# Gated expert rows of one token tile per pair: scaled by ScalarE and added by an accumulating DMA, instead of added by VectorE

## The chip, the cores and the metric

The kernel runs on one core of one Trainium2 chip. The metric is the device time of one execution in microseconds; the median of several executions is quoted. Those of the kernel before agree within 0.1 to 0.3%. A program on one core has no second die to be compared with, so every run here counts as "fast"; all of them are used. The profile takes one execution; its span is about 2 us shorter than the time.

Before the change: 989.57 us (median of 2 runs, 989.13 to 990.0).

## The reference, cut to what matters

A linear attention makes `x` (4608 tokens, 512 columns). Then every expert is applied to every token, weighted by a gate that a Sinkhorn iteration balances:

```python
out = np.zeros((N, D), dtype=np.float32)          # N, D, E, F = 4608, 512, 8, 1024
for e in range(E):
    h = np.maximum(x @ w1[e], 0.0)
    ye = h @ w2[e]
    out += P[:, e:e + 1] * ye                     # P: the balanced gates
```

The last line is what the change moves: a scaled addition of 512 columns per token and expert into an f32 output tile that stays in SBUF until the end.

## The kernel before

Experts 1 to 7 use a Strassen-like scheme with seven products in place of eight. Two instruction streams are woven together on TensorE: *groups* (the first matmul of the expert, 384 tokens wide, with results in the PSUM banks `X` = `h_ps`, `Y` = `copied_ps` and `Z` = `p7_ps`) and *pairs* (the second matmul, one pair of 128-token tiles `g1`, `g2` at a time). A `fill()` inside a group runs one step of a pair.

```python
    def group(hT, tw, xs, n, i, fill):
        ...
        X = ps_h[0].tile([P, TCH], FP32, name="h_ps")
        product(X, b11, x_part(0, 0, n), True)          # TensorE, 2 matmuls of 384 columns
        se.copy(out=Y[:, 0:TU], in_=X[:, 0:TU])         # ScalarE: X must be read before it grows
        fill()
        ...                                             # (last product of the group before)
        fill()
        product(X, T2, s2, False)                       # adds to X
        u2 = snapshot(X, "u2")                          # ScalarE again
        fill()
        product(Y, b21, x_part(0, 1, n), False)
        se.activation(out=h11, in_=Y[:, 0:TU], func=AF.Relu)
        fill()
        product(X, T1, s1, False)
        u4 = snapshot(X, "u4")
        ...
```

So three times in a group TensorE may not add to `X` before ScalarE has copied it out. A pair takes its seven steps at these places in the stream (seven places per pair), and gates its rows on VectorE:

```python
    OFFSETS = {"P1": 0, "P2": 3, "P7": 4, "P6": 5, "P4": 8, "P5": 9, "P3": 13}
    ...
        def add(self, g, rows, a=None):                 # class Pair
            ...
            a = acc(g) if a is None else a
            ve.scalar_tensor_tensor(
                out=a, in0=rows, scalar=P_tok[:, g, self.e : self.e + 1], in1=a,
                op0=ALU.mult, op1=ALU.add,
            )
        ...
            elif name == "P2":
                self.mult(self.W, self.a12, b21)
                self.add(self.g1, self.W, acc(self.g1)[:, 0:DH])     # half of the row, 256 columns
                ...
            elif name == "P3":
                self.mult(self.U, self.S4, b22)
                self.add(self.g1, self.U, acc(self.g1)[:, DH:Dm])    # the other half
                ...
```

The weights of the next expert come from GpSimd's DMA queue, since they are cast from f32 to f16 on the way, 1 MB (as written) at a time:

```python
            if n == 0 and e + 1 < E:
                w_next = new_weights(wA if e % 2 else wB)
                load_w1(w_next, e + 1, 1)
            if n == 2 and e + 1 < E:
                load_w2(w_next, e + 1, 1)
```

A scheduler puts the instructions of each engine into a fixed order when the program is built; TensorE's is tied to the written order, ScalarE's and VectorE's are not from expert 2 on. At run time each engine works through its own list in order.

## Time and profile before

| what | where it is read | number |
|---|---|---|
| TensorE busy in the stage of the pairs | busy time by window | 50.0 of 50 us |
| VectorE, ScalarE in the same stage | busy time by window | 43, 28 of 50 us |
| TensorE's share of the chain that ended last | chain of waits | 93% |
| TensorE waiting for gating adds | waits | 1.3 us in all |
| one pair | timeline | 6.1 us |

Busy time by engine, the first part of the profile page (busy us, share of the span, number of instructions):

```profile
PE 968.0 (98%) x7846; PEld 677.9 (69%) x7846; DVE 810.4 (82%) x1838; ACT 566.4 (57%) x1260; POOL 60.4 (6%) x82
```

Two stretches of 50 us of the stage that the change touches, from the view of busy time by window (us, then busy us and instructions of each engine, granted TensorE clock, DMA share, GB/s):

```profile
500.00:550.00 50.00, 49.98 (x384) 37.32 (x383) 43.01 (x102) 27.78 (x63) 0.75 (x1) 1.00 0.26 58
600.00:650.00 50.00, 49.98 (x383) 37.27 (x382) 43.16 (x103) 27.95 (x63) 0.75 (x1) 1.00 0.26 58
```

The first line of the chain that ended last, by engine:

```profile
PE 93%; DMA 2%; DVE 2%; ACT 1%; POOL 1%; issue 0%; DVEq 0%; POOLq 0%; ACTq 0%; SPq 0%
```

A VectorE that is busy 43 us of 50 looks like the engine to relieve. The waits view says which of the two waits for the other (engine, what it was to make, what it waited for: us in total, times, longest):

```profile
DVE acc_lo L814 <- PE rows_ps L109: 74.4, 77, 1.2
...
PE rows_ps L109 <- DVE acc_hi L814: 1.3, 3, 0.6
```

The gating adds wait 74 us for TensorE's rows, and TensorE waits 1.3 us for gating adds (all of it at `acc_hi`, the last four token tiles of the output; none at `acc_lo`). VectorE is used a great deal, and it is not what the time hangs on. The timeline (start, duration, engine, operation) around one `X` bank copy, with the lines of VectorE and of TensorE's own loading of weights (PEld) left out:

```profile
501.99 0.49 PE L109 MATMUL h_ps<-xT,w1e 128*128 128x384 f16 x2
502.32 0.60 PE L109 MATMUL rows_ps<-w2e,hs 128*128 128x256 f16 x4
502.57 0.46 ACT L763 COPY copied_ps<-h_ps 128x384 f32<-128x384 f32 x1 [0.33 <-PE h_ps L109]
502.75 0.49 PE L109 MATMUL p_ps<-xT,T 128*128 128x384 f16 x2
503.09 0.48 PE L109 MATMUL h_ps<-S,T 128*128 128x384 f16 x2
```

ScalarE's copy of `X` ends at 503.03 and TensorE's next product into `X` starts at 503.09. The starts of TensorE's products follow each other at 0.33 us (384 columns, two matmuls) and 0.43 us (256 columns, four), with no gap. ScalarE is busy only 28 us of 50, but in places like this one it has 0.06 us to spare.

The weight loads, from the list of DMA issues (KB each, median us from issue to landing):

```profile
w1e<-in_moe_w_dram POOLq DMA_DIRECT2D x7, 1024.0 KB, 9.3
w2e<-in_moe_w_dram POOLq DMA_DIRECT2D x7, 1024.0 KB, 10.0
```

### The profile page before, as it was taken

How to read it: one execution, taken by the hardware profiler on the slowest of the kernel's cores; microseconds unless marked ns; L12 is line 12 of the kernel's file. 1: busy time of each engine (PE TensorE's matmuls, PEld its weight loads, DVE VectorE, ACT ScalarE, POOL GpSimd, SP SyncE). 2: the span in 40 equal slices, each digit the busy share in tenths (PEclk: the TensorE clock that was granted, in tenths of full speed). 3: DMA queues.
4: the chain of work that ended last, by engine and by line, in shares of the span. 5: the costliest groups of instructions: out<-in, count | busy, mean ns of one | idle time of the engine just before them, and what ended most of it. 6: DMA issues, size and time to landing. Idle time of an engine off the chain costs nothing.

```text
span 987.4 us, 20228 instructions
## 1 busy us (share of the span) xinstructions
PE 968.0 (98%) x7846; PEld 677.9 (69%) x7846; DVE 810.4 (82%) x1838; ACT 566.4 (57%) x1260; POOL 60.4 (6%) x82
## 2 busy tenths in 40 slices
PE   7999999989999999999999999999999999999997
PEld 6445544447777777777777777777777777777775
DVE  5886774779889888988789888988789888988887
ACT  5756665467776555555555555555555555555551
POOL 6302110010000000000000000000000000000001
PEclk8999999999999999999999999999999999999999
DMA  9969981642013410133113400233103400104535
GB/s 168 206 99 154 160 153 26 125 67 67 26 48 68 75 42 25 38 79 67 42 33 68 88 29 25 51 66 68 49 25 68 92 25 27 48 25 114 131 86 128
DMA packets 80336, 73.54 MB, mean 74 GB/s; under 512 B 33264, under 2 KB 72176, under 8 KB 80240
## 3 DMA queue, kind: packets, MB, share of 16 engines
q0 software_dynamic: 27232, 30.94, 19.9%
q1 hardware_dynamic: 52768, 41.06, 16.9%
q8 instruction: 61, 1.00, 0.4%
q14 instruction: 35, 0.29, 0.1%
q10 hardware_dynamic: 240, 0.26, 0.1%
HBM read 83.12 MB, written 12.98 MB: 97 GB/s over the span
## 4 chain that ended last, share of the span: by engine, by line
PE 93%; DMA 2%; DVE 2%; ACT 1%; POOL 1%; issue 0%; DVEq 0%; POOLq 0%; ACTq 0%; SPq 0%
PE rows_ps L109 34%; PE h_ps L109 28%; PE copied_ps L109 11%; PE p_ps L109 11%; PE y_ps L109 5%; PE small_ps L109 4%; DMA v_ld<-in_v_dram 2%; DMA q_pT<-q_p 1%; DVE xT L109 0%; DVE acc_hi L814 0%; POOL hs_last L829 0%; DVE P_tok L109 0%; DMA out_dram<-acc_lo 0%; DVE colp L109 0%; ACT u L109 0%
## 5 line engine op out<-in xcount | busy, mean ns | idle before, releaser
L814 DVE SCALAR_TENSOR_TENSOR acc_lo<-rows_ps,P_tok,acc_lo 128x512 f32<-128x512 f32 (+1 forms) x322 | 203.7, 642 | 74.5 <-PE rows_ps L109 74.4
L109 PEld LDWEIGHTS <-H 128*128 128x128 f16 x2080 | 203.0, 98 | 83.1 <-issue 1.2
L750 ACT CAST u<-h_ps 128x384 f16<-128x384 f32 x288 | 137.8, 478 | 131.2 <-PE h_ps L109 130.6
L109 PEld LDWEIGHTS <-w1e 128*128 128x128 f16 x1632 | 156.3, 98 | 67.9 <-issue 7.8
L744 DVE CUSTOM_DVE_ANT_0 H<-p_ps,u 128x384 f16<-128x384 f32 x329 | 181.7, 552 | 6.6 <-PE p_ps L109 6.4
L109 PEld LDWEIGHTS <-hs 128*128 128x128 f16 x1500 | 146.6, 98 | 56.2
L109 PE MATMUL h_ps<-S,w1e 128*128 128x384 f16 x672 | 164.1, 326 | 1.1 <-ACT u L109 0.9
L109 PE MATMUL p_ps<-xT,T 128*128 128x384 f16 x672 | 164.1, 326 | 0.1
L109 PE MATMUL h_ps<-xT,w1e 128*128 128x384 f16 (+1 forms) x616 | 150.3, 351 | 1.4 <-DVE xT L109 1.3
L109 PE MATMUL rows_ps<-V,H 128*128 128x256 f16 x1000 | 150.0, 273 | 0.7 <-DVE acc_hi L814 0.7
L109 PE MATMUL rows_ps<-w2e,hs 128*128 128x256 f16 x1000 | 150.0, 273 | 0.0
L782 ACT ACTIVATE H<-h_ps 128x384 f16<-128x384 f32 x144 | 70.7, 491 | 95.0 <-PE h_ps L109 95.0
L109 PEld LDWEIGHTS <-T 128*128 128x128 f16 x1008 | 98.1, 98 | 29.2 <-issue 2.8
L109 PE MATMUL rows_ps<-w2e,H 128*128 128x256 f16 (+1 forms) x568 | 91.2, 285 | 0.0
L763 ACT COPY copied_ps<-h_ps 128x384 f32<-128x384 f32 x144 | 67.5, 468 | 35.2 <-PE h_ps L109 35.2
L773 ACT ACTIVATE H<-copied_ps 128x384 f16<-128x384 f32 x144 | 70.9, 492 | 20.3 <-PE copied_ps L109 20.3
L109 PE MATMUL h_ps<-S,T 128*128 128x384 f16 x336 | 81.8, 325 | 0.3 <-ACT copied_ps L109 0.3
L109 PE MATMUL copied_ps<-xT,w1e 128*128 128x384 f16 x336 | 82.1, 326 | 0.0
L109 PE MATMUL copied_ps<-w2e,H 128*128 128x256 f16 x504 | 75.5, 272 | 0.0
L109 PE MATMUL rows_ps<-V,hs 128*128 128x256 f16 x500 | 75.0, 272 | 0.0
L814 DVE SCALAR_TENSOR_TENSOR acc_lo<-copied_ps,P_tok,acc_lo 128x256 f32<-128x256 f32 x126 | 60.3, 479 | 0.4
L814 DVE SCALAR_TENSOR_TENSOR acc_hi<-rows_ps,P_tok,acc_hi 128x512 f32<-128x512 f32 (+1 forms) x56 | 41.3, 738 | 20.1 <-PE rows_ps L109 19.3
(135 smaller groups left out, 957.5 us busy)
## 6 DMA issues: line engine op xcount, KB each, us to landing
S<-x_saved SPq DMA_DIRECT2D x108, 192.0 KB, 2.4
out_dram<-acc_lo SPq DMA_DIRECT2D x62, 128.0 KB, 2.4
w1e<-in_moe_w_dram POOLq DMA_DIRECT2D x7, 1024.0 KB, 9.3
w2e<-in_moe_w_dram POOLq DMA_DIRECT2D x7, 1024.0 KB, 10.0
k_ld<-in_k_dram POOLq DMA_DIRECT2D x16, 288.0 KB, 8.4
v_ld<-in_v_dram POOLq DMA_DIRECT2D x16, 288.0 KB, 9.4
q_ld<-in_q_dram POOLq DMA_DIRECT2D x16, 288.0 KB, 7.8
x_saved<-S SPq DMA_DIRECT2D x18, 192.0 KB, 1.9
```

The lines of the kernel that those rows point to most:

```text
L109: i = getattr(self.engine, name)(*args, **kwargs)
L744: latest = ve._custom_dve(TENSOR_ADD_SAT, out=out, in0=ps[:, 0:TU], in1=t[:], s0=FP32_MAX, s1=0.0)
L750: se.copy(out=t[:], in_=ps[:, 0:TU])
L763: se.copy(out=Y[:, 0:TU], in_=X[:, 0:TU])
L773: se.activation(out=h11, in_=Y[:, 0:TU], func=AF.Relu)
L782: se.activation(out=h12, in_=X[:, 0:TU], func=AF.Relu)
L814: ve.scalar_tensor_tensor(out=a, in0=rows, scalar=P_tok[:, g, self.e : self.e + 1], in1=a, op0=ALU.mult, op1=ALU.add,)
```

## The change

The intent: take work from VectorE, the engine second in use. For experts 2 to 6, `g1` of each pair is no longer added by VectorE. ScalarE writes the gate times the rows into an SBUF tile `gated` (two buffers), and when both halves are there, a DMA from GpSimd's queue adds the tile to the output tile.

```diff
+    g_pool = ctx.enter_context(tc.tile_pool(name="g_pool", bufs=2))
...
+            self.by_dma = 1 < e < E - 1
...
+        def gate_half(self, cols, rows):
+            se.activation(
+                out=self.gated[:, cols], in_=rows, func=AF.Copy,
+                scale=P_tok[:, self.g1, self.e : self.e + 1],
+            )
...
             elif name == "P2":
                 self.mult(self.W, self.a12, b21)
+                if self.by_dma:
+                    self.gated = g_pool.tile([P, Dm], FP32, name="gated")
+                    self.gate_half(slice(0, DH), self.W)
+                    return
                 self.add(self.g1, self.W, acc(self.g1)[:, 0:DH])
...
             elif name == "P3":
                 self.mult(self.U, self.S4, b22)
+                if self.by_dma:
+                    self.gate_half(slice(DH, Dm), self.U)
+                    nc.gpsimd.dma_start(
+                        out=acc(self.g1), in_=self.gated[:], accum_op=ALU.add
+                    )
+                    return
                 self.add(self.g1, self.U, acc(self.g1)[:, DH:Dm])
```

## The prediction

> **What bounds the kernel now.** TensorE. In the stage that the change touches (expert pairs, about 240 to 980 us) the table of engine busy time by window shows TensorE 49.97 to 50.00 us busy in every 50 us, VectorE 41 to 45, ScalarE about 28, GpSimd 0 to 1.6. The chain of waits is 93% PE. The timeline shows its products (0.33 us for 384 columns, 0.43 for 256) back to back. In the waits view VectorE waits 94 us for row products and TensorE 1.3 us for the gating adds: relieving VectorE is worth at most a few us.
>
> **What the change removes, adds, moves.** 5 experts x 18 pairs = 90 pairs. Off VectorE: 180 adds of 128x256 at 0.48 us = 86 us (41-45 falls to about 36 per 50). Onto ScalarE: 180 scaled copies of 128x256, 0.36 us each like the present copy of that shape, = 65 us (28 rises to about 33 per 50). New: 90 accumulating 256 KB DMAs from GpSimd (+23.6 MB), one per 6.1 us. The PE order is unchanged.
>
> **What lies on the critical path.** The new loop through two buffers: the first scaled half of pair k+2 (step P2) waits in ScalarE's in-order queue until the DMA of pair k has landed. From the end of P3 of pair k to the end of P2 of pair k+2 the present timeline gives 3.4 to 3.7 us; less the copy (0.37) about 3.0 us remain for the DMA.
> The DMA: present weight loads start their first packet 1.5 to 1.7 us after GpSimd's issue and take 0.17 us per 2 KB row; 8 rows per engine 1.4 us, plus receipt and semaphores 0.5: about 3.6 us (estimate), more if accumulating slows the rows. The Trainium skill, "DMA: Bandwidth & Descriptors", "Anatomy of one DMA", gives 2.0 us + bytes/436e3 = 2.6 us for a plain copy; no run shows it yet. So ScalarE is blocked perhaps 0.6 to 0.9 us per pair, up to 2 us with slow accumulation. TensorE feels it where a snapshot of the h bank follows: those have only 0.1 or 0.5 us of slack. Estimate: 5 to 90 us in all, central 25.
> Second: the weight loads share GpSimd's queue (one only, by "SWDGE vs HWDGE vs iDMA" there). They take 9.4 and 10.4 us to land; a P3 comes 1.7 us after a w1 load's issue and another just after a w2 load's. Those accumulations wait behind 1 MB; ScalarE blocks 5 to 8 us, eight times (4 w1 + 4 w2): about 40 us.
>
> **Prediction.** 1055 us, range 1005 to 1130. Faster by over 2%: 0.01; within 2%: 0.12; slower by over 2%: 0.87.
>
> **What would show it.** (1) VectorE busy falls by some 86 us and its idle time grows: no gain. (2) ScalarE waits for the DMA into the output tile: a new entry, tens of us, with the longest single waits 5 us or more, just after weight issues. (3) Landing of the accumulation: median 3 to 5 us, maximum over 9. (4) TensorE idle waiting for ScalarE (the h-bank copies and snapshots), some 60 us in experts 2 to 6; matmuls per 50 us fall from 384 to about 355 there, and stay 384 in expert 7.
>
> **What would make it wrong.** If the accumulation lands in under 3 us and isn't held behind weight data (rings interleaving), the time stays 985 to 1000. If accumulating runs at a fraction of copy speed, a landing of 6 us or more would cost over 150 us. A scheduled order that puts each blocked copy where ScalarE has nothing urgent would hide most of it.

## The result

1081.89 us (median of 2 runs, 1078.65 to 1085.13) against 989.57. The ratio is 1.0933, with a 95% interval from 1.0791 to 1.1075: slower by 9%. (Here and below, a ratio is the mean time of one kernel's fast runs over the mean of the other's of the same rounds, so it isn't quite the ratio of the medians quoted.) The result of the kernel is correct.

Busy time by engine, after:

```profile
PE 993.3 (92%) x7846; PEld 684.3 (64%) x7846; DVE 758.2 (70%) x1658; ACT 626.6 (58%) x1440; POOL 137.7 (13%) x172
```

VectorE has 180 instructions fewer and ScalarE 180 more, as intended. VectorE's busy time fell by 52 us and not by the 86 predicted: adds that stand back to back with other work overlap it by some 0.2 us each, and overlapping time is counted once. The plain sum of the durations of its instructions, without those that only wait, fell by 86 us (from 925 to 840).

Stretches of the stage, after (the columns as before). The last one is in expert 7, where nothing was changed:

```profile
450.00:500.00 50.00, 41.62 (x295) 29.73 (x293) 28.02 (x56) 25.25 (x60) 6.08 (x7) 0.93 0.46 86
600.00:650.00 50.00, 45.15 (x330) 32.76 (x330) 29.99 (x60) 30.91 (x74) 6.81 (x8) 0.97 0.35 74
1000.00:1050.00 50.00, 50.00 (x385) 37.46 (x384) 39.94 (x87) 27.92 (x63) 0.00 (x0) 1.00 0.46 113
```

TensorE does 295 to 330 matmuls in 50 us where it did 384, and the granted clock is below 1.00 in these stretches. In expert 7 both are as before. The new waits:

```profile
ACT gated L822 <- DMA acc_lo<-gated: 95.4, 64, 7.3
...
PE h_ps L109 <- ACT copied_ps L764: 46.5, 35, 6.4
...
PE h_ps L109 <- ACT u L751: 18.8, 8, 5.7
```

ScalarE, about to write a `gated` tile, waits 95 us for the DMA that still reads that buffer; TensorE, about to add to `X`, waits 65 us for ScalarE's copies. The scaled copy itself, from the costliest groups (count, then busy us and mean ns of one, then idle time before them). These are the first halves, which wait for the buffer; the 90 second halves also take 476 ns each:

```profile
L822 ACT ACTIVATE gated<-copied_ps,P_tok 128x256 f32<-128x256 f32 x90 | 42.7, 474 | 114.7 <-DMA acc_lo<-gated 95.4
```

The DMA in the list of issues:

```profile
acc_lo<-gated POOLq DMA_DIRECT2D x90, 256.0 KB, 3.6
```

And its shortest, median and longest landing, from the view of the tile `gated`:

```profile
DMA to landing us min/median/max: 3.2/3.6/11.3
```

The timeline of one of the long stalls shows the whole mechanism (lines picked out, in order of time; many between them are left out):

```profile
425.99 0.78 POOL L127 DMA_DIRECT2D w1e<-in_moe_w_dram  x1 [3.10 <-PE h_ps L109]
428.02 0.85 POOL L900 DMA_DIRECT2D acc_lo<-gated  x1 [1.25 <-ACT gated L822]
432.62 0.60 PE L109 MATMUL rows_ps<-w2e,hs 128*128 128x256 f16 x4
436.89 0.47 ACT L822 ACTIVATE gated<-copied_ps,P_tok 128x256 f32<-128x256 f32 x1 [5.41 <-DMA acc_lo<-gated]
437.26 0.47 ACT L751 CAST u<-h_ps 128x384 f16<-128x384 f32 x1
437.79 0.80 PE L109 MATMUL h_ps<-S,w1e 128*128 128x384 f16 x2 [4.57 <-ACT u L751]
...
442.95 0.49 PE L109 MATMUL h_ps<-S,T 128*128 128x384 f16 x2
```

A weight load is issued at 426.0 and an accumulation at 428.0, which lands only 8.8 us later. ScalarE, blocked for 5.4 us on the buffer, can't get to the snapshot `u` behind it in its list, and TensorE stands still for 4.6 us. Then comes something that I had not thought of: the two matmuls after the stall take 0.80 us instead of 0.49. They run at half clock, and at 442.95 the old duration is back.

TensorE's list is the same in both kernels, so its matmuls can be compared one by one. From the starts of all matmuls in the two traces, I set out how much later TensorE is at the end of the change's stage than before (88.4 us):

| part of the 88.4 us | us |
|---|---|
| 8 gaps of 3.4 to 6.7 us between successive matmuls, one per weight load | 41 |
| 37 gaps of 0.4 to 2.0 us | 30 |
| matmuls at half clock: spacing of about 0.32 and 0.21 us instead of 0.163 and 0.107 | 15 |
| rest | 3 |

The trace's record of the granted clock has eight stretches at 0.5 in this stage, each of 3.4 or 6.8 us, one at the end of each of the eight long gaps. Part of each lies in the gap itself, where it costs nothing, so 44 us at half clock cost 15.

### The profile page after: what moved, and what is told of

The parts are those of the page before. It is cut to its first block, busy times and chain, and to the rows that moved or that the text cites. A ratio compares the mean times of both kernels' runs of the same rounds, so it can differ in the third digit from the quotient of the medians.

```text
span 1076.7 us, 20630 instructions
## 1 busy us (share of the span) xinstructions
PE 993.3 (92%) x7846; PEld 684.3 (64%) x7846; DVE 758.2 (70%) x1658; ACT 626.6 (58%) x1440; POOL 137.7 (13%) x172
## 4 chain that ended last, share of the span: by engine, by line
issue 47%; PE 38%; POOL 7%; DMA 3%; DVE 3%; ACT 2%; POOLq 0%; ACTq 0%; DVEq 0%
PE h_ps L109 12%; PE rows_ps L109 10%; POOL acc_lo L900 6%; PE y_ps L109 5%; PE small_ps L109 4%; PE copied_ps L109 3%; PE p_ps L109 3%; DMA acc_lo<-gated 2%; DMA k_ld<-in_k_dram 1%; DVE acc_lo L816 0%; POOL w1e L127 0%; DVE xT L109 0%; ACT gated L822 0%; DVE hs L837 0%; DVE acc_hi L816 0%
## 5 line engine op out<-in xcount | busy, mean ns | idle before, releaser
L816 DVE SCALAR_TENSOR_TENSOR acc_lo<-rows_ps,P_tok,acc_lo 128x512 f32<-128x512 f32 (+1 forms) x232 | 163.2, 707 | 139.6 <-PE rows_ps L109 138.9
L109 PEld LDWEIGHTS <-H 128*128 128x128 f16 x2080 | 205.5, 99 | 87.6 <-issue 6.0
L109 PE MATMUL h_ps<-S,w1e 128*128 128x384 f16 x672 | 168.1, 332 | 20.1 <-ACT u L751 18.8
L109 PE MATMUL p_ps<-xT,T 128*128 128x384 f16 x672 | 166.3, 330 | 0.0
L900 POOL DMA_DIRECT2D acc_lo<-gated x90 | 77.1, 857 | 519.2 <-ACT gated L822 471.0
L822 ACT ACTIVATE gated<-copied_ps,P_tok 128x256 f32<-128x256 f32 x90 | 42.7, 474 | 114.7 <-DMA acc_lo<-gated 95.4
```

Of the source, the lines that this page charges most:

```text
L109: i = getattr(self.engine, name)(*args, **kwargs)
L816: ve.scalar_tensor_tensor(out=a, in0=rows, scalar=P_tok[:, g, self.e : self.e + 1], in1=a, op0=ALU.mult, op1=ALU.add,)
L822: se.activation(out=self.gated[:, cols], in_=rows, func=AF.Copy, scale=P_tok[:, self.g1, self.e : self.e + 1],)
L900: nc.gpsimd.dma_start(out=acc(self.g1), in_=self.gated[:], accum_op=ALU.add)
```

## The experiments

**Theory A.** TensorE has no time to spare and VectorE's relief is worth nothing. Two `gated` buffers leave a DMA about 3 us to land. It lands in 3.6 us, so ScalarE blocks a little in most pairs (the 30 us); behind a weight load it lands in 8 to 11 us, so ScalarE blocks for long (the 41 us). **Theory B.** ScalarE's 180 extra copies, or the 23.6 MB more of DMA traffic, cost the time directly. **Theory C**, for the part that the prediction lacked: a long stall of TensorE halves its clock for a while.

### 1. Four buffers (e1_bufs4)

```diff
-    g_pool = ctx.enter_context(tc.tile_pool(name="g_pool", bufs=2))
+    g_pool = ctx.enter_context(tc.tile_pool(name="g_pool", bufs=4))
...
-            pool = u_pool if self.last else hs_pool          # 6 KB of u_pool serve one pair only
+            if self.last:                                    # make room: borrow two idle buffers
+                lend = [g_pool.tile([P, Dm], FP32, name="gated")[:].bitcast(F16) for _ in range(2)]
+                ...
```

Two more buffers need room in SBUF. The last pair's `hs_last` tiles now borrow `gated` buffers.

> Four buffers of the scaled rows instead of two (the room comes from tiles of the last pair, which borrow two of them). Theory A (ScalarE waits in its queue for a buffer, that is for the landing of the DMA two pairs back): with four buffers a DMA has 3.4 + 2 x 6.1 = some 15 us, more than its longest landing of 11.3 us, so ScalarE's 95 us of waiting for the landing goes to under 5 us, TensorE's waits for ScalarE from 65 us to under 8 us, granted clock back to 0.995, time 989 to 1000 us. Theory B (the time is ScalarE's 86 us of extra copies, or the DMA traffic itself slowing memory): stays above 1050 us.

Measured: 989.66 us (4 runs), ratio 1.0003 (0.9988 to 1.0018). The new wait of ScalarE for the landing isn't in the list any more. TensorE's stretch from 600 to 650 us, from busy time by window:

```profile
600.00:650.00 50.00, 50.00 (x384) 37.30 (x383) 38.69 (x88) 33.32 (x79) 7.88 (x10) 1.00 0.52 100
```

384 matmuls again, at full clock. ScalarE does all its added work (33 us busy of 50, where it was 28), the DMA engines move all the added bytes, and landings are as long as before (3.2/3.6/10.7 us). So neither the work nor the traffic costs time: what cost it was the wait for a buffer. Theory B falls. And the time isn't below that of the kernel before, although VectorE has 4 to 5 us more of idle time in each 50: its relief is worth nothing. (One caveat: the scheduler also moved eight of ScalarE's scaled copies one or two places forward in its list, just at the eight weight loads. The traces show this same new order in e1, e2, e3, e5, e6, e7 and e9; only e4 and e8 keep the changed kernel's list. Two runs with this order and two buffers, e5 and e9, still take 1049 and 1037 us, so the order alone did not gain the time.)

### 2. The scaled copies without the DMA (e2_no_dma)

```diff
                     self.gate_half(slice(DH, Dm), self.U)
-                    nc.gpsimd.dma_start(
-                        out=acc(self.g1), in_=self.gated[:], accum_op=ALU.add
-                    )
                     return
```

> The scaled copies stay on ScalarE, the accumulating DMA is left out (two buffers; the result is wrong on purpose: experts 2 to 6 are missing for half of the rows). Theory A: nothing waits for a landing, so the time is 989 to 1000 us although ScalarE does all the added work and VectorE none of the removed. Theory B, in its form that ScalarE's extra copies cost the time: above 1050 us. A gain over the kernel before (under 980 us) would show that VectorE's relief is worth something; theory A says it is not, at most 3 us.

Measured: 990.48 us (4 runs), ratio 1.0011 (0.9996 to 1.0026). This agrees with theory A on both sides: the copies alone cost nothing, and a VectorE with some 85 us less to do gains nothing.

### 3. The same bytes as a plain copy on another queue (e3_plain_sync)

```diff
-                    nc.gpsimd.dma_start(
-                        out=acc(self.g1), in_=self.gated[:], accum_op=ALU.add
-                    )
+                    nc.sync.dma_start(
+                        out=acc(self.g1), in_=self.gated[:]
+                    )
```

> The same bytes at the same place in the program with two buffers, but as a plain copy on SyncE's hardware queue, away from the weight loads' queue (the result is wrong on purpose: overwritten instead of added). Theory A with the shared queue: landing median about 2.7 us as 192 KB loads on that queue take 2.6, and no long landing behind a weight load (maximum under 6 us), longest ScalarE wait under 3 us, clock 0.99 or more, time 992 to 1010 us. Rival (the weight load saturates the 16 DMA engines, whatever the queue): landings near weight loads still 8 us or more, eight stalls remain, time above 1040 us.

Measured: 1022.27 us (4 runs), ratio 1.0330 (1.0312 to 1.0349). This is a miss of the upper bound (1010), and an instructive one. The ordinary landing is 2.3 us, and the ordinary loss is gone (TensorE's delay hardly grows between the stalls). But four stalls remain, all at w1 loads, with a longest landing of 8.0 us on a queue that has no weight load in it. First the landing from the view of the tile, then lines picked from the timeline:

```profile
DMA to landing us min/median/max: 2.2/2.3/8.0
...
419.95 0.75 POOL L127 DMA_DIRECT2D w1e<-in_moe_w_dram  x1 [83.68 <-DVE T L723]
421.71 0.47 SPq L900 DMA_DIRECT2D acc_lo<-gated  x1
429.64 0.47 ACT L822 ACTIVATE gated<-copied_ps,P_tok 128x256 f32<-128x256 f32 x1 [5.00 <-DMA acc_lo<-gated]
430.54 0.80 PE L109 MATMUL h_ps<-S,T 128*128 128x384 f16 x2 [4.91 <-ACT copied_ps L764]
...
453.08 0.88 POOL L133 DMA_DIRECT2D w2e<-in_moe_w_dram  x1 [32.38 <-DVE acc_lo L816]
453.32 0.47 SPq L900 DMA_DIRECT2D acc_lo<-gated  x1
```

The packets in the trace tell more. The rows of the w1 load start at 421.4. The copy, issued at 421.7, has none of its 128 rows started before 425.7, and half of them not before 427.1, when three quarters of the load's rows have started. Other copies show rows starting about 1.1 us after the issue. From 425.7 on, rows of both appear side by side, and the copy even lands before the load. At the w2 load (453.08) the copy was issued 0.24 us later, and its rows started first, at 454.5 against 455.3: it landed in 3.0 us. So a shared *queue* isn't needed for a long wait: the four copies behind w1 loads took 7.5 to 8.0 us on a queue of their own. What delays them is a load that reached the shared *DMA engines* first.

The queue still matters, because it decides who comes first. Experiment 7 issues the same plain copy from GpSimd, and there the w2 load and the copy stand like this:

```profile
453.51 0.90 POOL L133 DMA_DIRECT2D w2e<-in_moe_w_dram  x1 [5.44 <-PE rows_ps L109]
454.40 0.55 POOL L900 DMA_DIRECT2D acc_lo<-gated  x1
```

The copy can be issued only when GpSimd has issued the load, 0.9 us later, and the four copies behind w2 loads land in 9.3 to 10.3 us there, against 2.9 to 3.0 here. With eight long stalls instead of four, that kernel takes 1052 us and not 1022. (ScalarE's order differs between the two as well, as said in experiment 1.) The Trainium skill ("DMA: Bandwidth & Descriptors", "Issuing engines are not separate DMA queues") says that DMAs run on the same 16 engines whichever engine started them; the copies behind w1 loads agree, with 7.5 to 8.0 us on a separate queue against 7.7 to 8.7 us in experiment 7 on the shared one. The section "Queues, rings and completion order" has each engine take turns between queues by packets of typically 9 to 17 descriptors and at most 64. A load here has 512 rows, 32 for each of 16 DMA engines, which would be one turn only near that limit; no run here shows the packets' limits, so why the copy's first rows came only 4 us after its issue stays open.

### 4. Useless matmuls in the stalls (e4_busy)

```diff
+        if 2 < e < E - 1 and (n, i) == (1, 3):
+            busy(28)                     # 28 matmuls of 384 columns into Z, which is rewritten next
         product(X, T2, s2, False)
...
+        if 2 < e < E - 1 and (n, i) == (0, 1):
+            busy(20)
         product(X, T1, s1, False)
```

The places are those of the eight long gaps. The lists of VectorE, ScalarE and GpSimd are the same as in the changed kernel, instruction by instruction.

> The changed kernel with useless matmuls put into TensorE's order just before the two matmuls per expert (experts 3 to 6) at which it stalls longest: 20 of 384 columns (3.3 us) and 28 (4.6 us), 32 us of work in all; everything else in the same order. Theory C (a stall of 3 us or more halves the granted clock for 3.4 to 6.8 us after it, some 20 us of the loss): TensorE no longer idles long, no half-clock stretch in the stage, clock 0.99 or more, and the time FALLS by 10 to 20 us to 1060 to 1072 us although TensorE does more. Rival (half clock follows from the DMA burst or from power, or costs nothing): clock stays near 0.975 and the time stays at 1080 us or rises by up to 10.

Measured: 1068.44 us (4 runs), ratio to before 1.0802 (1.0784 to 1.0820), so 13 us faster than the changed kernel, with more work. The granted clock is 0.997 over the run, and no stretch at half clock is left in the stage. ScalarE's wait for the landings is the same (97.7 us against 95.4). The matmuls ran inside the stall:

```profile
466.19 4.71 PE L109 MATMUL p_ps<-xT 128*128 128x384 f16 x28 [0.21 <-DVE H L753]
471.55 0.48 PE L109 MATMUL h_ps<-S,T 128*128 128x384 f16 x2 [0.64 <-ACT copied_ps L772]
```

After the stall a pair of matmuls takes 0.48 us here, not 0.80. Theory C holds: it is TensorE's own idle time that halves its clock. The gaps shrank by 28 us and 31 us of useless work came in, so without an effect of the clock the run would have lost 3 us. With the 15 us of half clock in the count above it should gain 12 us; it gained 13.

The traces of all eleven runs also say when the clock is halved. It changes only at the steps of a grid of 3.413 us that runs through a whole trace, whatever TensorE does. Between 300 us and the last tens of us of each trace, 2176 such windows began at full clock. TensorE was idle for 2.04 us or more in 23 of them, and each of these was followed by half clock; in all others it was idle for at most 1.97 us, and none was. (The ends of matmuls are modelled, so the border is good to a tenth or so.) What counts is how much of one window a gap fills, not how long the gap is: one of 3.7 us from start to start in experiment 8 fell as 1.8 and 1.7 us into two windows and cost no clock.

### 5. The same useless matmuls where there is no stall (e7_bufs4_busy)

The edit of experiment 4 in the four-buffer kernel.

> Control for the useless matmuls: the same 192 of them put into the four-buffer kernel, where TensorE has no stall for them to fill. Theory C: they cost their full time there, 192 x 0.163 = 31 us over the four-buffer kernel: 1018 to 1024 us, whereas in the two-buffer kernel the same matmuls made it 13 us faster. If they are nearly free here too, the argument from them falls.

Measured: 1022.35 us (4 runs), ratio to before 1.0326. That is some 32 us over the four-buffer kernel (1.0326 against 1.0003), full price (192 x 0.163 = 31 us). The same instructions made the two-buffer kernel 13 us faster, so they are not cheap; they stood in time that was lost anyway.

### 6. Three buffers (e6_bufs3)

The edit of experiment 1 with `bufs=3`.

> Three buffers. Theory A: a DMA has about 9.1 us instead of 3.0 before ScalarE needs its buffer, more than the usual 3.6 us, less than the 10.4 to 11.3 us behind a w2 load. So the ordinary waits vanish and at most four short ones of 1 to 2 us are left, with no half clock: 990 to 998 us. If instead the gain of four buffers came from the shifted places of the copies in ScalarE's order, three would lie anywhere between.

Measured: 996.01 us (4 runs), ratio 1.0054 (1.0039 to 1.0070). From the waits view:

```profile
ACT gated L822 <- DMA acc_lo<-gated: 10.9, 5, 2.8
...
PE h_ps L109 <- ACT copied_ps L764: 4.3, 4, 1.6
```

Five waits are left, of at most 2.8 us; TensorE has five gaps of 1.0 to 1.8 us and no half clock in the stage. With 95 us, 11 us and no wait for two, three and four buffers, the loss goes as the time that a buffer leaves the DMA: about 3, 9 and 15 us. ScalarE's list is in the same order with three and four buffers, so a change of its order would not give different losses here.

### 7. Plain copy from GpSimd (e8_plain_pool)

```diff
-                        out=acc(self.g1), in_=self.gated[:], accum_op=ALU.add
+                        out=acc(self.g1), in_=self.gated[:]
```

> The changed kernel with a plain copy instead of the accumulation, still from GpSimd (the result is wrong on purpose). The rows of the plain copy on SyncE took 0.085 us, those of the accumulation 0.184 us. Theory A: rows at 0.09 us make the landing 0.8 us shorter, 2.8 us, less than the 3.0 us that a pair has, so the ordinary loss of 26 us all but goes (under 8 us), the eight stalls behind weight loads stay nearly as long: 1045 to 1062 us. If GpSimd's way of issuing and not the accumulation is the slow part, the landing stays near 3.5 us and the time above 1068 us.

Measured: 1051.97 us (4 runs), ratio 1.0623 (1.0597 to 1.0649). The landing from the view of the tile:

```profile
DMA to landing us min/median/max: 2.2/2.3/10.3
```

So accumulating costs 1.3 us of the 3.6: GpSimd takes 0.86 us to issue it and 0.54 for the copy, and a 2 KB row takes about 0.19 us in place of 0.085 (here packets of 4 KB at 0.171), eight rows per DMA engine. With 2.3 us to land the copy is in time in most pairs: the gaps of under 2.5 us sum to 12 us instead of 30. The eight long gaps stay (36 us), and the half clock with them.

### 8. Weight loads in four pieces (e5_split)

```diff
+                if 1 < e < E - 1 and n in (1, 3):            # after each of a unit's four groups
+                    (load_w1 if n == 1 else load_w2)(w_next, e + 1, 4, i)   # piece i of 4
...
-                load_w1(w_next, e + 1, 1)
+                if e == 1:
+                    load_w1(w_next, e + 1, 1)
...                                                          # load_w2 alike; each piece waits for
                                                             # the last VectorE result of its group
```

> The changed kernel, two buffers and the accumulating DMA from GpSimd as they are, but the weight loads of experts 4 to 7 (and 3) cut into four pieces of 256 KB that are held to one piece per group, 4.6 us apart, instead of 1 MB at once. Theory A (a burst of weight data ahead of the accumulation on the DMA engines makes the long landings): a piece takes some 1.4 us of the engines, so the longest landing falls from 11.3 to under 6 us, no stall of TensorE over 2.5 us is left, the clock stays at 0.99 or more, and of the 92 us about 62 go: 1017 to 1032 us, what is left being the ordinary wait of each pair. Rival (the amount of weight traffic counts, not the burst): as before the edit, above 1060 us.

Measured: 1048.94 us (4 runs), ratio 1.0584 (1.0564 to 1.0604): a miss by 17 us, though far from the rival's. The landing, from the view of the tile:

```profile
DMA to landing us min/median/max: 3.2/3.4/7.2
```

Gaps of over 2.5 us fell from eight (41 us) to four (11 us), and half clock from 44 us to 10. What I had left out is that the 40 pieces now delay many accumulations a little (landings of 4.4 to 7.2 us in 13 places), which added 11 us to the small gaps. The edit also moved the loads of expert 3 into the stage, where there were accumulations for them to delay; until 435 us the gaps sum to 9 us, where the changed kernel has 5. In a loop with no slack, cutting a burst up took away part of the delay and spread another part.

### 9. Weight loads right after an accumulation (e9_phase)

```diff
                     d = nc.gpsimd.dma_start(
                         out=acc(self.g1), in_=self.gated[:], accum_op=ALU.add
                     )
+                    if held_loads:
+                        not_before(d, held_loads.pop(0)())   # a whole 1 MB load, next on the queue
```

> The changed kernel with two buffers; the eight weight loads of experts 4 to 7 stay whole (1 MB) and on GpSimd's queue, but each is issued right after an accumulation instead of just before one. Bytes, queue and burst are the same, only the order changes. Theory A': what counts is that an accumulation issued in the first 2 us of a 1 MB load stands behind all of it. Now the next one comes 6.1 us later and finds 3 to 4 us of the load left: landing 4.5 to 5.7 us there instead of 8 to 11, eight stalls of 1 to 2 us instead of 3.4 to 6.7, no half clock in the stage, 1024 to 1040 us. Rival (any MB of weights costs a stall of the same length, whatever the order): above 1065 us. The split loads (a miss: 1049 us against 1017 to 1032 expected) left open which of the two holds.

Measured: 1037.50 us (4 runs), ratio 1.0483 (1.0462 to 1.0505). The landing, from the view of the tile:

```profile
DMA to landing us min/median/max: 3.2/3.6/5.6
```

And ScalarE's wait for it:

```profile
ACT gated L824 <- DMA acc_lo<-gated: 60.5, 62, 2.7
```

Same bytes, same queue, same bursts, two buffers: issuing each load just behind an accumulation instead of just ahead of one takes 44 us off. The next accumulation comes 6 us later, when most of the load is through. The longest gap is 2.5 us, and the stage has no half clock at all.

No version tried beats the kernel before. With four buffers the change ties, because TensorE's list sets the time of this stage in both.

## Why the prediction was right, point by point

The measured 1081.89 us lies within the range of 1005 to 1130, and "slower by over 2%", given 0.87, came true.

- *TensorE is the bound, VectorE's relief is worth at most a few us*: right. The four-buffer kernel and the one without the DMA have the relief without the wait, and stand at 1.0003 and 1.0011 of the time before.
- *Two buffers leave about 3.0 us, the accumulation takes about 3.6 us, more if accumulating slows the rows*: right in the sum, and partly by luck. The median landing is 3.6 us. But the 0.17 us per row was that of the weight loads; a plain copy within SBUF takes 0.085 us and lands in 2.3 us, which would not have blocked ScalarE in most pairs. Accumulating does slow the rows, to 0.19 us, which is close to the figure that was borrowed.
- *ScalarE's copies take 0.36 us*: wrong in size. They take 0.474 us. The figure was that of the copy of the same shape into PSUM; these go to SBUF, with a scale.
- *Ordinary loss 25 us*: 30 us in 37 gaps. Right.
- *Loss behind weight loads 40 us in eight places of 5 to 8 us of blocking*: 41 us in eight gaps of 3.4 to 6.7 us. Right in size; the reason given was half right. The prediction put it down to the shared queue. Behind w1 loads the copies on SyncE's own queue took 7.5 to 8.0 us just the same: there the shared DMA engines and the order of arrival are enough. Behind w2 loads the own queue did remove the wait (2.9 to 3.0 us), because the copy could overtake the load.
- *Total 1055 us*: 27 us short. The sum was 25 + 40, and TensorE's waits for ScalarE do amount to 65 us. What was missing is that TensorE comes out of a long stall at half clock: 15 us by the matmul spacings, confirmed by the useless matmuls. The rest of the 27 us is some 6 us of larger gaps, 3 us not placed, and 3 us by which the median lies above the run that was profiled. The fourth sign named in the prediction, about 355 matmuls per 50 us, came out lower (295 to 366, on average 331 from 330 to 989 us), in part for that reason.
- *VectorE busy falls by 86 us*: 86 us by the sum of durations, 52 us as the page counts.

## What to carry to other kernels

Before taking work from the busiest helper engine, ask which engine waits for which: at 82% busy VectorE was waiting for TensorE, so its relief was worth nothing. A result that leaves by DMA needs enough buffers for the time in which one is filled plus the *longest* landing, not the median one. Here a buffer is filled for 9.1 us (from the first scaled half to the end of the second, with four buffers) and a pair comes every 6.1 us: 9.1 + 11.3 us are 3.3 periods, so four buffers. Two cost 9%, three cost 0.5% and four nothing, with the same work. And where an in-order engine serves both a slow consumer and the critical engine, one wait for the former becomes a stall of the latter, and a stall that leaves TensorE idle for over 2.0 us of one clock window of 3.4 us costs again in half clock.

## What the Trainium skill lacked or had wrong

- "TensorE: Matmul & The Clock Gate", Part 1, has the clock halve after at least one idle window of about 3.4 us. Here a window that was idle in part was enough: in the run with split loads, gaps of 2.3, 2.4 and 2.7 us were each followed by 3.4 us at half clock. All 23 windows with 2.04 us or more of idle time were followed by half clock, and none with up to 1.97 us was (experiment 4). That the windows are free-running, as the page says, agrees: the clock changed on a fixed grid of 3.413 us, and a gap of 2.5 us in the run with moved loads and one of 3.7 us in the run with split loads, which fell across two windows, had no effect. The half clock lasted whole windows, 3.4 or 6.8 us.
- "DMA: Bandwidth & Descriptors" says that an accumulating DMA must be issued from GpSimd but has no duration for one. Here a 2 KB f32 row took 0.19 us accumulating within SBUF against 0.085 us copying, the issue 0.86 us against 0.54, the landing of 256 KB 3.6 us against 2.3.
- The same page's formula for GpSimd's DMAs ("Anatomy of one DMA", 2.0 us + bytes/436e3) gives 2.6 us for a plain 256 KB; measured 2.3 us within SBUF, from GpSimd and from SyncE alike. For the accumulation it would be 1.0 us short.
- The same page, "Queues, rings and completion order", lets a reader expect that two queues share a DMA engine by turns. A 256 KB copy on SyncE's queue had none of its rows started until 4.2 us after a 1 MB load on GpSimd's queue had begun, and landed in 7.8 us instead of 2.3; after that the rows of both did run side by side. The page has no number for how long one queue can be held up by another.
